# A spectral mixer and a Mish MLP on one core: early dense blocks on half chunks, loads reordered, planner given tile shapes and POOL durations

## The chip, the core and the metric

The kernel runs on one core of one Trainium2 chip. The metric is the time of one execution in microseconds as the device counts it, median over runs. The engines are PE (TensorE, matmuls; its weight loads are shown as PEld), DVE (VectorE), ACT (ScalarE), POOL (GpSimd) and SP (SyncE, which here only issues transfers). Transfers are issued from SP, ACT and POOL. PSUM, where PE writes, has eight banks of 512 float32 columns.

## The reference

Both branches read the same `x`, 2048 x 512 in bf16; a gate per row mixes them.

```python
x = A_x
g = _sigmoid((x * gate_w).sum(-1, keepdims=True))
a = _A_ref(x, A_w_r, A_w_i)     # irfft2(rfft2(x) * (w_r + 1j * w_i)), bf16
b = _B_ref(x, B_w1, B_b1, B_w2) # h = x @ w1 + b1 (512 -> 1792); act = h * tanh(softplus(h)); act @ w2
return g * a + (1 - g) * b
```

## The kernel before

**Tiling.** The 2048 rows are 16 tiles of 128 rows, in four chunks of four. `xo` holds the tiles as loaded, `xT` their transposes (made by PE against `ident`, L539, and copied out of PSUM by the tasks `evx`, L543). Everything stays in on-chip memory but two round trips of the spectral branch through DRAM (`scr1`, `scr2`).

**Dense branch.** For each chunk c and each of 14 blocks of 128 hidden units (ft), task `mm1_c_ft` is four matmuls of 512 columns (L861) into one PSUM bank, `mish` (L875, ACT) applies the activation out of that bank, and `mm2` (L892) multiplies by `w2`. The four blocks ft = 0 to 3 of chunk 0 ("early") are split in two tasks of two matmuls, `a` and `b`, by the halves of the contraction, because their `w1` comes in two pairs of loads (`ld_w1_a`, `ld_w1_b`). `DENSE` and `DENSE2` list the banks that mm1 and mm2 of a chunk may use.

**Spectral branch.** `t` (L561) forms sums and differences of `xT` into `Tb` (part of the buffer `Tg`) for a chunk; `a1` (L577) transforms along the row with the table `FDs` (load `ld_fd`); `eg`, `e1` (L584 to L595) combine into `Abuf`; `s1` (L608) is the first half of the transform down the columns, with 64-row tiles of PE and the tables `m1g1`; `e2` evicts to `Ybuf`, and `r1w` stores to `scr1`, one half issued from SP, the other from POOL. `r1r` (`Abuf<-scr`) reads back; `s2c`, `s2` (L704, L749: 64 rows by 32 columns), products with the spectral weights `WT` (`wm`, `wz`), `s2i` (L780: 32 by 64), stores and loads through `scr2`, then `s1i`, `a1i` (L809, L821) and the last sums. Small things on the side: `wcols` (POOL, L645) takes columns of `WT`, `rcw` (PE, L654), `weff` (DVE), `wab1` and `wab2` (POOL, L667 to L682) make a table from them; `gdot`, `gpow` (POOL, L631), `gcol`, `omg` make the gate.

**The order is made by a planner.** Every piece of work is a task with an engine, a duration, what it reads and writes, and a priority. `schedule()` walks through simulated time and picks among the ready tasks by priority plus a seeded noise (`SEED`, `MORE`). `LAND` gives times at which the first loads are taken to land. The result is one fixed order for each engine; each engine runs its order strictly in turn, and waits on semaphores where a task needs another engine's result. So a late input holds up everything that stands behind it on that engine. The planner's durations are assumptions: they set the order, not the time.

**The start.** The idle matmuls `warm` (L484) multiply constants while the first loads come in; nothing reads their result. The loads of tiles 0 to 3 are issued first, alternately from SP and ACT, then the first pair of `w1`, `b1`, `FD`, the second pair of `w1`, and the larger ones (tiles 4 and 5, tiles 6 and 7, `w1` blocks 4 to 7, ...).

Of the kernel before, what the change touches and what calls it, by code (L numbers as in the profile page):

```python
# [7 lines left out]
BF = mybir.dt.bfloat16  # L8
F32 = mybir.dt.float32
AF = mybir.ActivationFunctionType  # L10
ALU = mybir.AluOpType
# [105 lines left out]
class _Task:  # L117
    __slots__ = ("name", "eng", "dur", "fn", "deps", "lat", "sem", "semval", "idx", "sig",
                 "start", "done", "succ", "bl", "prio", "xfer", "opts", "isdma", "alloc", "frees", "lock", "nd")

    def __init__(self, name, eng, dur, fn, lat=0.0, prio=0.0):
# [20 lines left out]
        self.lock = False  # L142


SCH = dict(eps=0.03, sync=0.05)
# [3 lines left out]
class _Graph:  # L149
# [49 lines left out]
    def schedule(self):  # L199
# [26 lines left out]
        left = len(tasks)  # L226
        while left:
# [45 lines left out]
            ready.remove(t)  # L273
            t.start = est
# [48 lines left out]
S1N = 2  # L323
S1B = [(6, 7), (4, 5), (2, 3)]
A1B = (3, 4, 5, 6, 7)
SEED = 102926
NOISE = 0.02
MORE = (906649, 669565, 727213, 734900, 722035, 224221, 575189, 474236, 545212, 216745, 750436, 520841, 226433, 475143, 916690, 739973, 998134, 850898, 920291, 410068, 968422, 18581, 591859, 602267, 674493, 703441, 110116, 413622, 829488, 66903, 591144, 731731, 191705, 399980, 537679, 776088, 374283, 444805, 454649, 718084, 219781, 617544, 95571)
# [5 lines left out]
LAND = dict(ld_x0=2.9, ld_x1=3.1, ld_x2=3.7, ld_x3=4.0, ld_w1_a0=4.9, ld_w1_a1=5.0,  # L334
            ld_b1=6.6, ld_fd=5.6, ld_w1_b0=6.2, ld_w1_b1=6.2, ld_x4=9.0, ld_x6=9.0,
            ld_w1_4_0=10.0, ld_w1_4_1=10.6, ld_x8=12.1, ld_m10=13.1, ld_x12=14.4, ld_w1_8_0=15.3,
            ld_w1_8_1=16.0, ld_m11=17.3, ld_w1_12_0=17.7, ld_w1_12_1=18.1, ld_gw=18.5, ld_sm=19.0,
            ld_gd=19.3)
# [3 lines left out]
def _build(nc, A_x, A_w_r, A_w_i, B_x, B_w1, B_b1, B_w2, gate_w, out):  # L342
# [8 lines left out]
    with es:  # L351
# [128 lines left out]
        one_w, one_m = (nc.const_aps.tensor(1.0, (128, n), BF) for n in (128, 256))  # L480
        pw = _Ps([6])
        tw = []
        for i in range(NWARM):
            tw.append(pe(f"warm{i}", mm(256), lambda e: e.matmul(ps[:, pw.bank, 0:256], one_w, one_m, start=True, stop=True),  # L484
                         alloc=pw if i == 0 else None, frees=[pw], prio=0.0, deps=tw[-1:]))
# [46 lines left out]
        for t0, w in ((0, 1), (1, 1), (2, 1), (3, 1), (4, 2), (6, 2), (8, 2), (10, 2), (12, 2), (14, 2)):  # L532
            pt = _Ps(SPEC[::-1])
            def f_tr(e, t0=t0, w=w, pt=pt):
                ins = None
                for i in range(w):
# [8 lines left out]
                  reads=[("ptr", t0)], writes=[("xT", t0 + i) for i in range(w)], frees=[pt], engs=("dve",), prio=PR["tr"] + max(0, 4 - t0) * 0.2)  # L545
# [10 lines left out]
        for t in range(NT):  # L556
            if t % 4 == 0:
                G.cur_prio = PR["sp"] + 0.9
                h = t // 4
                cols = slice(512 * h, 512 * h + 512)  # L560
                for (nm, o, op) in (("s", 0, ALU.add), ("d", 2, ALU.subtract)):  # L561
                    tt(f"t{nm}{h}", lambda o=o, hb=h % 2: Tb[:, hb, o:o + 2, :], lambda cols=cols: xT[:, 0:2, cols],
                       lambda cols=cols: xT[:, 2:4, cols], op, 1024, rate=2.0,
                       reads=[("xT", 4 * h + i) for i in range(4)], writes=[("T", h % 2, nm)])
            if t % 2 == 0:
# [3 lines left out]
                for half in range(2):  # L569
# [11 lines left out]
                    pe(f"a1{half}_{t}", 4 * mm(128), f_a1, reads=[("T", hb, "s"), ("T", hb, "d"), "FD"], writes=[("pa", t, half)], alloc=pa,  # L581
# [14 lines left out]
            if t % 4 == 3:  # L596
                p1s = [_Ps(S1B) for _ in range(2)]
                for qd in range(0, 2, S1N):
# [13 lines left out]
                    s1_tasks.append(pe(f"s1_{tps[0]}", 4 * S1N * mm(256) + 0.22, f_s1, reads=[("In1" + x, tp) for tp in tps for x in "pmf"] + [("m1g1", t // 8)],  # L612
                                       writes=[("p1", tp) for tp in tps], alloc=p1s[qd:qd + S1N], prio=PR["sp"] + 0.4))
                for tp, p1 in zip((t - 3, t - 1), p1s):
# [3 lines left out]
                    for rho in range(2):  # L618
                        dma(f"r1w{tp}{'ab'[rho]}", scr1_w[rho][:, 2 * tp:2 * tp + 4, :], Y1[rho::2, 2 * tp:2 * tp + 4, :], reads=[("Y1", tp)],
                            writes=[("scr1", tp, rho)], nbytes=64 * 4 * 512, prio=PR["sp"] + 1.0, tail=0.7, bw=290e3, queue=("sp", "pool")[rho], issue=0.64)  # L620
# [10 lines left out]
        G.add("gpow", "pool", 0.3, lambda e: e.tensor_tensor(out=gcol[:, :], in0=omg[:, :], in1=gdot[:, :], op=ALU.pow),  # L631
# [32 lines left out]
        G.add("weff", "dve", 0.4, f_weff, reads=["pW"] + WALL, writes=["wq"], frees=[pW])  # L664
# [19 lines left out]
        G.add("wab2", "pool", 1.2, f_wab2, reads=["ch"], writes=["wab"], lock=True)  # L684
# [23 lines left out]
        pe("s2c", 0.6, f_s2c, reads=[("In2", r, u) for r in range(2) for u in range(8)] + ["sm"], writes=["pc"], alloc=pc)  # L708
# [29 lines left out]
        for v in range(4):  # L738
            u0, zb = 2 * v, v % 2
            q_of = {}  # L740
            for c in range(2):
# [11 lines left out]
                pe(f"s2_{v}{c}", mm(512) + 0.2, f_s2, reads=[("In2", r, u0 + i) for r in range(2) for i in range(2)] + ["sm"],  # L753
# [30 lines left out]
            t_s2i = pe(f"s2i_{v}", 2 * mm(512) + 0.25, f_s2i, reads=[("Z", zb, 2)] + [("Z", zb, r, c) for c in range(2) for r in range(2)] + ["sm"],  # L784
# [66 lines left out]
        for c in range(NCH):  # L851
            hb = c % 3
            G.cur_prio = PR["mm1"] - c
            for ft in range(NFT):
# [3 lines left out]
                def f_mm1(e, c=c, ft=ft, pd=pd, ds=range(4)):  # L858
                    ins = None
                    for i in ds:  # L860
                        ins = e.matmul(ps[:, pd.bank, :], w1_sb[:, i, 128 * ft:128 * (ft + 1)], xT[:, i, 512 * c:512 * c + 512],  # L861
                                       start=(i == 0), stop=(i == 3))
# [164 lines left out]
```

## Time and profile before

| what | us |
|---|---|
| median of 3 runs (131.64, 132.22, 132.03) | 132.03 |
| the profiled execution | 131.42 |
| its span, first to last instruction | 129.7 |
| PE busy in it | 126.3 |
| DVE, ACT, POOL busy | 87.8, 73.1, 63.8 |
| span of the last matmul's end to the span's end | 2.3 |

The granted TensorE clock is full in the mean over the span. The busy time of each engine by stretch of the span (PE, PEld, DVE, ACT, POOL; the counts in brackets are instructions; then the granted clock, the mean share in which the DMA engines were busy, and GB/s):

```profile
4.80:6.07 1.27, 1.05 (x12) 0.67 (x12) 1.23 (x5) 0.46 (x2) 0.00 (x0) 1.00 1.03 338
6.07:9.97 3.90, 3.88 (x30) 1.98 (x30) 1.59 (x4) 1.75 (x3) 0.00 (x0) 1.00 0.95 282
9.97:42.20 32.23, 32.23 (x266) 18.16 (x266) 29.11 (x59) 25.38 (x43) 10.74 (x21) 1.00 0.87 257
42.20:52.78 10.58, 10.54 (x50) 4.61 (x48) 4.57 (x14) 8.53 (x13) 7.67 (x12) 1.00 0.57 172
52.78:93.00 40.22, 40.22 (x307) 16.00 (x308) 23.56 (x22) 18.69 (x26) 21.76 (x25) 1.00 0.44 144
93.00:127.40 34.40, 34.40 (x269) 20.06 (x266) 26.98 (x56) 17.24 (x34) 22.43 (x30) 1.00 0.21 80
```

The first stretch is the end of the start-up, the second the first dense blocks, the third the rest of the forward spectral stage with dense work between, the fourth the round trip through `scr1`, the fifth the middle of the spectral branch, and the last the inverse transform with `mm2` between. A busy PE here counts pipelined matmuls that overlap, so the stretches are read by their lengths. DVE and ACT are busiest in the third.

### The profile page before, as it was taken

The numbers are of one execution on the slowest core, as the hardware profiler recorded it, in microseconds if no ns is written. First come the engines' busy times: TensorE is split into PE (matmuls) and PEld (weight loads), VectorE is DVE, ScalarE is ACT, GpSimd is POOL, SyncE is SP. The second block draws the span as 40 slices with busy tenths as digits, with TensorE's granted clock in tenths as the row PEclk, the third lists the DMA queues.
The fourth block names the chain that finished last, engine by engine and source line by source line (L and its number), as shares of the span: only waits on it lengthen the run. The fifth ranks groups of instructions, "written<-read, shape, count | busy, mean of one in ns | idle before, by whom it ended". The sixth has DMA issues, their size and how long they took to land.

```text
span 129.7 us, 2516 instructions
## 1 busy us (share of the span) xinstructions
PE 126.3 (97%) x948; PEld 64.3 (50%) x948; DVE 87.8 (68%) x157; ACT 73.1 (56%) x120; POOL 63.8 (49%) x97
## 2 busy tenths in 40 slices
PE   7999999999999999999999999999999999999992
PEld 5655756544455444344343333344556666555452
DVE  0638897988999921581698994600248987798672
ACT  0456567889887877604056857922245636743320
POOL 3000009800157994049579979200009887977820
PEclk9999999999999999999999999999999999999999
DMA  3999963999976645937014050465920030024213
GB/s 100 315 273 419 376 206 68 365 290 223 233 206 194 174 124 153 407 107 303 5 34 130 0 162 5 126 197 138 407 102 5 30 134 0 5 81 164 81 40 121
DMA packets 14584, 21.09 MB, mean 163 GB/s; under 512 B 1324, under 2 KB 10796, under 8 KB 14188
## 3 DMA queue, kind: packets, MB, share of 16 engines
q1 hardware_dynamic: 12288, 14.80, 34.3%
q0 software_dynamic: 1248, 4.99, 14.4%
q10 hardware_dynamic: 1036, 1.15, 2.8%
q8 instruction: 7, 0.11, 0.4%
q14 instruction: 5, 0.04, 0.1%
HBM read 14.64 MB, written 6.29 MB: 161 GB/s over the span
## 4 chain that ended last, share of the span: by engine, by line
PE 86%; DMA 5%; POOL 4%; DVE 1%; ACT 1%; issue 1%; SPq 0%
PE ps L892 37%; PE ps L861 29%; DMA Abuf<-scr 3%; PE ps L809 3%; PE ps L577 3%; PE ps L821 3%; PE ps L539 3%; PE ps L484 2%; POOL wab L674 2%; PE ps L608 2%; PE ps L749 2%; PE ps L780 2%; DMA scr<-Ybuf 2%; POOL scr L429 1%; DVE xT L459 1%; ACT Ybuf L460 1%
## 5 line engine op out<-in xcount | busy, mean ns | idle before, releaser
L861 PE MATMUL ps<-xT,w_sb 128*128 128x512 bf16 x224 | 52.8, 380 | 0.2 <-DVE xT L459 0.2
L892 PE MATMUL ps<-w_sb,act 128*128 128x512 bf16 (+2 forms) x238 | 51.6, 367 | 0.0
L875 ACT ACTIVATE act<-ps,b1f 128x512 bf16<-128x512 f32 x56 | 38.4, 687 | 15.0 <-PE ps L861 11.8
L892 PEld LDWEIGHTS ps<-w_sb,act 128*128 128x128 bf16 x238 | 21.9, 98 | 22.3 <-issue 0.6
L861 PEld LDWEIGHTS ps<-xT,w_sb 128*128 128x128 bf16 x224 | 19.9, 98 | 25.1 <-issue 2.6
L464 POOL TENSOR_TENSOR Tg<-Qb 128x256 bf16<-128x256 f32 x30 | 22.4, 773 | 19.9 <-DVE Qb L832 19.6
L464 POOL TENSOR_TENSOR Zb<-Qb 128x510 bf16<-128x510 f32 x16 | 19.8, 1267 | 8.3 <-DVE Qb L464 8.3
L464 DVE TENSOR_TENSOR Qb<-ps,WT 128x1024 f32<-128x1024 f32 x16 | 18.8, 1218 | 7.2 <-PE ps L749 4.1
L842 ACT ACTIVATE xo<-ps,omg 128x512 bf16<-128x512 f32 x14 | 9.6, 687 | 21.3 <-PE ps L892 20.5
L832 DVE SCALAR_TENSOR_TENSOR Qb<-ps,gcol,Qb 128x256 f32<-128x256 f32 x32 | 13.7, 475 | 3.0 <-PE ps L809 1.0
L464 DVE TENSOR_TENSOR Abuf<-ps,Tg 128x512 bf16<-128x512 f32 x16 | 10.3, 687 | 2.8 <-ACT Tg L584 2.2
L459 DVE CAST Ybuf<-ps 128x1024 bf16<-128x1024 f32 x8 | 9.8, 1222 | 3.3 <-PE ps L780 2.9
L459 DVE CAST Zb<-ps 128x512 bf16<-128x512 f32 x6 | 4.1, 688 | 11.5 <-PE ps L809 11.2
L826 ACT ACTIVATE Qb<-ps,gcol 128x256 f32<-128x256 f32 x16 | 7.3, 472 | 7.0 <-PE ps L821 7.0
L626 DVE SCALAR_TENSOR_TENSOR Tg<-xo,Tg 128x512 bf16<-128x512 bf16 x16 | 11.0, 686 | 0.4
L429 POOL DMA_DIRECT2D scr<-Ybuf x8 | 5.1, 645 | 12.0 <-ACT Ybuf L460 12.0
L429 POOL DMA_DIRECT2D w_sb<-in_B_w_dram x2 | 2.1, 1059 | 17.6 <-DMA sm<-c_sm 17.6
L460 ACT ACTIVATE Ybuf<-ps 128x1024 bf16<-128x1024 f32 x8 | 8.2, 1024 | 4.4 <-PE ps L780 3.3
L459 DVE COPY xT<-ps 128x1024 bf16<-128x1024 bf16 (+1 forms) x10 | 5.5, 582 | 5.3 <-PE ps L539 5.1
L464 DVE TENSOR_TENSOR xo<-xo,Tg 128x512 bf16<-128x512 bf16 x14 | 8.6, 644 | 0.6 <-POOL Tg L464 0.6
L821 PEld LDWEIGHTS ps<-GDs,Zb 128*128 128x128 bf16 x64 | 4.6, 98 | 2.6 <-DVE Qb L832 0.3
L821 PE MATMUL ps<-GDs,Zb 128*128 128x128 bf16 x64 | 5.9, 219 | 0.0
(68 smaller groups left out, 89.1 us busy)
## 6 DMA issues: line engine op xcount, KB each, us to landing
Abuf<-scr SPq DMA_DIRECT2D x8, 512.0 KB, 5.4
scr<-Ybuf SPq DMA_DIRECT2D x4, 512.0 KB, 3.2
w_sb<-in_B_w_dram POOLq DMA_DIRECT2D x2, 896.0 KB, 6.8
out_dram<-xo SPq DMA_DIRECT2D x6, 256.0 KB, 2.0
WT<-in_A_w_r_dram POOLq DMA_DIRECT2D x4, 257.0 KB, 9.0
WT<-in_A_w_i_dram POOLq DMA_DIRECT2D x4, 257.0 KB, 12.6
w_sb<-in_B_w_dram SPq DMA_DIRECT2D x4, 256.0 KB, 8.0
xo<-in_A_x_dram SPq DMA_DIRECT2D x2, 512.0 KB, 8.3
```

The costliest lines, as they stand in the source:

```text
L429: t = G.add(name, queue, issue, lambda e: e.dma_start(dst, src), reads=reads, writes=writes, lat=tail, deps=deps, prio=prio)
L459: fs = {"dve": ("dve", dve_dur(n, rate=rate), lambda e: e.tensor_copy(out=dst(), in_=src())), "act": ("act", act_dur(n), lambda e: e.activ ...
L460: "act": ("act", act_dur(n), lambda e: e.activation(dst(), src(), AF.Copy))}
L464: f = lambda e: e.tensor_tensor(out=o(), in0=i0(), in1=i1(), op=op)
L626: lambda e, t=t: e.scalar_tensor_tensor(out=junk, in0=xo[:, t, :], scalar=1.0, in1=gwb, op0=ALU.mult, op1=ALU.mult, accum_out=gdot[:, t:t ...
L821: ins = e.matmul(ps[:, p5.bank, 128 * i:128 * i + 128], TT[:, sl, 2 * par + ri, :], GDs[:, i, :], start=True, stop=True)
L826: lambda e, t=t, sl=sl, p5=p5: e.activation(gC[:, sl, :].rearrange("p (i n) -> p i n", i=2), ps[:, p5.bank, :].rearrange("p (i n) -> p i n ...
L832: lambda e, t=t, sl=sl, p5=p5, o=o, op=op: e.scalar_tensor_tensor(out=st1[:, sl, o::2, :], in0=ps[:, p5.bank, :].rearrange("p (i n) -> p i ...
L842: G.add_multi(f"bev_{t}", [("act", act_dur(512, True), lambda e: e.activation(xo[:, t, :], ps[:, pd.bank, :], AF.Copy, scale=omg[:, t:t + ...
L861: ins = e.matmul(ps[:, pd.bank, :], w1_sb[:, i, 128 * ft:128 * (ft + 1)], xT[:, i, 512 * c:512 * c + 512], start=(i == 0), stop=(i == 3))
L875: lambda e, ft=ft, pd=pd, hb=hb: e.activation(act[:, hb, ft, :].rearrange("p (t a b) -> p t a b", t=4, b=2), ps[:, pd.bank, :].rearrange(" ...
L892: ins = e.matmul(ps[:, pd.bank, cs_], act[:, hb, ft, 128 * tl:128 * (tl + 1)], w2_sb[:, ft, cs_], start=(ft == 0), stop=(ft == NFT - 1))
```

## The change

It has five parts.

1. **Early dense blocks by halves of the chunk.** Each of the four early blocks becomes four tasks of two matmuls with 256 columns: `a0`, `b0` (tiles 0 and 1) and `a1`, `b1` (tiles 2 and 3). They need only their two tiles. The sums and differences `t` of the first chunk are split in the same way, and `a1` waits for its half. Tiles 2 and 3 may be evicted by ACT too.
2. **Load order.** Tiles 0 and 1, the first pair of `w1`, tiles 2 and 3, the second pair of `w1`, then `b1` (ACT) and `FD` (SP). What follows is as before.
3. **Idle matmuls.** 36 of 128 columns, not 17 of 256.
4. **The planner.** It knows which tasks use other tile shapes of PE (`MODES`): it adds 0.095 us where the shape changes, prefers a task of the same shape that is nearly ready, and the allowances in the durations of `s1`, `s2`, `s2c`, `s2i` go. `gpow`, `wab2` and `weff` get 3.0, 3.1 and 0.9 us where they had 0.3, 1.2 and 0.4. `LAND`, the seeds and the assumed tail of the `r1w` stores are new.
5. **Banks.** mm1 of chunk 3 may use banks 0, 1 and 7, where it had 0 and 1; the first four transposes go through banks 4 to 7.

```diff
+MODES = {"s1": 1, "s2": 2, "s2c": 2, "s2i": 3}
+SWITCH = 0.095
...
+            stay = [c for c in cand if c[2][2] == "pe" and c[1].mode == mode and mode and c[0] <= free["pe"] + 0.15]
+            if stay:
+                cand = [c for c in cand if c[2][2] != "pe"] + stay
...
+            if t.eng == "pe" and t.mode != mode:
+                mode = t.mode
+                est += SWITCH
...
-DENSE = {0: (0, 1, 2), 1: (0, 1), 2: (0, 1, 7), 3: (0, 1)}
+DENSE = {0: (0, 1, 2), 1: (0, 1), 2: (0, 1, 7), 3: (0, 1, 7)}
...
-NWARM = 17
+NWARM = 36
...
-        one_w, one_m = (nc.const_aps.tensor(1.0, (128, n), BF) for n in (128, 256))
+        one_w, one_m = (nc.const_aps.tensor(1.0, (128, n), BF) for n in (128, 128))
...
-        for t in range(4):
+        for t in range(2):
             ld_x(t, t + 1, both[t % 2])
         ld_w1c(0)
+        for t in range(2, 4):
+            ld_x(t, t + 1, both[t % 2])
+        ld_w1c(1)
         dma("ld_b1", braw[:, :], B_b1.rearrange("(ft p) -> ft p", p=128), writes=["braw"], nbytes=3584, queue="act")
         dma("ld_fd", FDs[:].rearrange("p r k -> p (r k)"), d_FD[:], writes=["FD"], nbytes=131072)
-        ld_w1c(1)
...
-            pt = _Ps(SPEC[::-1])
+            pt = _Ps((7, 6, 5, 4) if t0 < 4 else SPEC[::-1])
...
-                  reads=[("ptr", t0)], writes=[("xT", t0 + i) for i in range(w)], frees=[pt], engs=("dve",), prio=PR["tr"] + max(0, 4 - t0) * 0.2)
+                  reads=[("ptr", t0)], writes=[("xT", t0 + i) for i in range(w)], frees=[pt], engs=("dve", "act") if t0 in (2, 3) else ("dve",), prio=PR["tr"] + max(0, 4 - t0) * 0.2)
...
+                for js in (((0,), (1,)) if h == 0 else ((0, 1),)):
+                    j0, nj = 256 * js[0], 256 * len(js)
+                    cols = slice(512 * h + j0, 512 * h + j0 + nj)
...
-        G.add("gpow", "pool", 0.3, lambda e: e.tensor_tensor(out=gcol[:, :], in0=omg[:, :], in1=gdot[:, :], op=ALU.pow),
+        G.add("gpow", "pool", 3.0, lambda e: e.tensor_tensor(out=gcol[:, :], in0=omg[:, :], in1=gdot[:, :], op=ALU.pow),
...
-        G.add("wab2", "pool", 1.2, f_wab2, reads=["ch"], writes=["wab"], lock=True)
+        G.add("wab2", "pool", 3.1, f_wab2, reads=["ch"], writes=["wab"], lock=True)
...
-                    t_a = pe(f"mm1_{c}_{ft}a", 2 * mm(512), lambda e, f=f_mm1: f(e, ds=(0, 1)), reads=xs + wr[0], alloc=pd, prio=PR["mm1"] - 0.06 * ft)
-                    pe(f"mm1_{c}_{ft}b", 2 * mm(512), lambda e, f=f_mm1: f(e, ds=(2, 3)), reads=xs + wr[1], writes=[("pm", c, ft)], deps=[t_a],
-                       prio=PR["mm1"] + 0.5 - 0.06 * ft)
+                    t_a = None
+                    for j in range(2):
+                        for h in range(2):
+                            tk = pe(f"mm1_{c}_{ft}{'ab'[h]}{j}", 2 * mm(256), lambda e, f=f_mm1, h=h, j=j: f(e, ds=(2 * h, 2 * h + 1), j0=256 * j, j1=256 * j + 256),
+                                    reads=xs[2 * j:2 * j + 2] + wr[h], writes=[("pm", c, ft, j)], alloc=None if t_a else pd, deps=[t_a] if t_a else (),
+                                    prio=PR["mm1"] + 0.8 * j + 0.3 * h - 0.06 * ft)
+                            t_a = t_a or tk
```

What the new plan makes of it, as the built programs have it (names of before in brackets where a line number would differ):

```
PE before: warm x14, transposes of tiles 0-3, warm x3, dense 512 x6, transpose of b1, dense x2, a1 x16, dense x4,
           transposes of tiles 6, 7 x8, dense x2, of tiles 4, 5 x8, dense x10, of tiles 8-11, ...
PE after:  warm x26, transposes of tiles 0, 1, warm x10, dense 256 x4, transposes of tiles 2, 3, dense 256 x6, a1 x8,
           transpose of b1, dense 256 x6, a1 x8, dense 256 x12, transposes of tiles 4-7, dense 256 x4, dense 512 x8,
           of tiles 8-11, dense x4, s1 x16 (L608), transposes of tiles 12-15, ...
s1 blocks: before, all four follow the transposes and the last a1; after, the first one as above, the others as before.
PE between the last s1 block and the first s2: before 48 dense matmuls; after rcw (L654) and 48 dense.
Dense (mm1) matmuls of 512 columns ahead of the first s2: before 164; after 156, two halves counted as one.
POOL before: w2 x2, WT x8, r1w x4, wcols, r1w x2, wab1, wab2, r1w x2, gpow, ...
POOL after:  r1w x2, w2 x2, WT x8, r1w x2, wcols, r1w x4, wab1, wab2, gpow, ...
```

More of the change, by code (lines that the diff above doesn't have):

```diff
@@ L782, in f_s2i @@
                 return ins
[L784 removed]
+            t_s2i = pe(f"s2i_{v}", 2 * mm(512) + 0.04, f_s2i, reads=[("Z", zb, 2)] + [("Z", zb, r, c) for c in range(2) for r in range(2)] + ["sm"],
                writes=[("p3", v)], alloc=p3)
@@ L877, in _build @@
                                                                           AF.Mish, bias=b1f[:, ft:ft + 1]),
-                      reads=[("pm", c, ft), "b1f"], writes=[("act", hb, ft)], frees=[pd], prio=PR["mish"])
+                      reads=([("pm", c, ft, j) for j in range(2)] if early else [("pm", c, ft)]) + ["b1f"], writes=[("act", hb, ft)], frees=[pd], prio=PR["mish"])
             G.cur_prio = PR["mm2"] - c
```

48 lines of the change are left out of this document (25 added, 23 removed).

## The prediction

> **What bounds the kernel now.** I read the page first: one engine is busy throughout.
>
> ```profile
> span 129.7 us, 2516 instructions
> PE 126.3 (97%) x948; PEld 64.3 (50%) x948; DVE 87.8 (68%) x157; ACT 73.1 (56%) x120; POOL 63.8 (49%) x97
> ```
>
> A busy PE need not be a PE at its rate, so next came the chain of waits in order of time (start, length, what).
>
> ```profile
> 0.83 3.15 PE ps L484 x14
> 3.98 0.44 PE ps L539 x4
> ...
> 4.87 1.16 DVE xT L459 x3
> 6.03 0.04 issue
> 6.07 1.47 PE ps L861 x6
> ...
> 9.97 0.62 PE ps L539 x8
> ...
> 27.37 3.45 PE ps L861 x16
> ...
> 42.66 3.06 POOL wab L674 x7
> 45.72 0.65 POOL scr L429
> 46.37 2.21 DMA scr<-Ybuf
> ...
> 48.66 4.08 DMA Abuf<-scr
> 52.74 0.04 issue
> 52.78 0.63 PE ps L749 x16
> ...
> 75.42 4.60 PE ps L861 x20
> ```
>
> Sixteen dense matmuls take 3.45 us, so 0.216 us each, and PE holds that rate nearly everywhere. What it loses lies in four places. (1) The start: nothing useful but sixteen transposes runs before 6.07, because the first dense block needs all four tiles evicted by DVE. (2) At 9.97, where transposes wait for a load. (3) At 52.78: the 48 dense matmuls in front began at 42.21, 48 x 0.216 = 10.37 gives 52.58, and the chain there runs through POOL and two transfers; of the 0.20 lost, 0.10 is the change of tile shape (below) and 0.10 the wait. (4) Small holds: twenty matmuls at 75.42 take 4.60, not 4.32. A block before a change of tile shape costs 0.10 more (eight take 1.83 at 33.76, in front of L608, and 1.73 at 17.81); the other 0.18 are two holds, and the timeline of the weight loads names the releaser, three times in this stretch.
>
> ```profile
> 70.33 0.55 PEld L861 LDWEIGHTS ps<-xT,w_sb 128*128 128x128 bf16 x4 [0.41 <-ACT act L875]
> ...
> 77.17 0.55 PEld L861 LDWEIGHTS ps<-xT,w_sb 128*128 128x128 bf16 x4 [0.41 <-ACT act L875]
> ...
> 78.98 0.55 PEld L861 LDWEIGHTS ps<-xT,w_sb 128*128 128x128 bf16 x4 [0.41 <-ACT act L875]
> ```
>
> So the kernel is a string of PE work from 6.07 to 127.4, and a change is worth what it takes off the front or out of the string. The list of loads gives the arrival times.
>
> ```profile
> FDs<-c_fd SPq DMA_DIRECT2D x1, 128.0 KB, 3.9
> xo<-in_A_x_dram ACTq DMA_DIRECT2D x1, 256.0 KB, 6.6
> ```
>
> FD is issued at 2.17 and lands at 6.11; tiles 6 and 7 are issued at 3.29 and land at 9.92. The landing events give the rest: tiles 0 and 1 at 3.59 and 3.79, 2 and 3 at 4.78 and 5.08, the first w1 pair at 5.53 and 5.74, the second at 6.45 and 6.77, w1 blocks 4 to 7 at 11.28.
>
> **The change, part by part.** *Idle matmuls.* Fourteen of 256 columns last from 0.83 to 3.77, 0.210 each; 26 of 128 columns take 26 x 0.105 = 2.73 and end at 3.56. Tile 0 lands at 3.59, so its transposes start near 3.60, 0.17 earlier. Evictions follow as before: the second ended at 4.87 + 0.42 = 5.29, now 5.12, and PE starts 0.06 later (as 6.01 to 6.07): first dense matmul at 5.18. The first w1 pair must be there: it takes the queue places of tiles 2 and 3, 5.08. The ten idle matmuls in between (three slow, seven at 0.056, from 4.46) end at 5.17 and cost nothing. So dense work starts 0.89 earlier, but eight transposes (tiles 2, 3) now stand behind it: 8 x 0.056 = 0.45. Lead 0.44.
>
> *Halved early matmuls.* 16 more matmuls and weight loads. Four 128-column ones take 0.22 against 0.216 for one of 512, under 0.003 for each extra start: 0.04 in all. The extra weight loads (0.098 each) hide under matmuls of 0.109; where that cover is thinner, in the 0.056 transposes, they hide too.
>
> *Load order.* The second w1 pair is now seventh and eighth of the 128 KB loads, FD ninth. The eighth landed at 6.45, the tenth at 6.77. PE wants w1 at 5.18 + 0.44 + 0.45 + 0.44 = 6.51 and FD at 6.73. Bounds 0 to 0.26 of waiting; I take 0.05, since the places say 6.45 and between 6.45 and 6.77. DVE's four half-size sums (0.35 each, from 5.12) end at 6.5 and are covered too; one eviction moves to ACT, idle then.
>
> *The next loads cap the lead.* Up to tiles 6 and 7 PE has 14 half pairs x 0.219, 8 + 16 transposes and line transforms x 0.056 and 0.21 for the small transpose = 4.63; 5.18 + 4.63 + 0.05 = 9.86. Tiles 6 and 7 land at 9.92, so these transposes start at 9.97 again. Before, PE had done 12 full dense matmuls by then and waited 0.18; now 14. Lead 2 x 0.216 = 0.43, less 0.01 for the halves left: 0.42. Then w1 blocks 4 to 7 are needed at 11.30 and land at 11.28. Both loads stand where they stood, with the same bytes ahead. Bounds 0.34 (PE 0.26 late) to 0.47.
>
> *The order behind.* The built program has the same groups of each tile shape (four of L608, nine of the others), so the knowledge of shapes saves no change of 0.10: nothing. The first L608 block moves up to before the last transposes; DVE must have made its input by 14.9. From 4.3 it has about 9.0 us to do (its operations at 0.61, the half-size ones at 0.35), end 13.3; if not, PE waits in order and everything behind it. POOL's wab now stands behind the stores: 3.06 off a chain that had missed by 0.10; the loads land some 3 us early. Gain 0.10. The last dense chunk gets a third bank: the three holds go, 0.26 (bounds 0 to 0.26). Chunk 1 keeps two banks, and ACT has an extra eviction (1.02) and copies before it: I allow two holds of 0.09, 0.17 (bounds 0 to 0.26). Behind 127.41 nothing changes.
>
> Sum: -0.42 - 0.10 - 0.26 + 0.17 = -0.61 (the cost of the halves is in the 0.219). The profiled execution took 131.42, its span 129.7 and 1.7 around it, and the median of the runs is 0.61 above that. So 131.42 - 0.61 = 130.81 for an execution like the profiled one, and on the median 132.03 - 0.61 = **131.4**.
>
> **Rivals.** *B, the good ends.* Start 0.47, wait 0.10, holds 0.26 and none new: -0.83, 131.2. For it: ACT runs its evictions 0.59 apart back to back (7.96, 8.55), so it need not be late. Against: two loads must land sooner than they did.
>
> *C, PE still slow when dense work begins.* The transposes of tile 1 ran 0.107 apart, those of tile 2, at 4.82, 0.056: the clock rose at 4.81, and dense now starts only 0.37 later. Had it risen later, the old kernel would hardly mind before 6.07; the new one loses half of each us from 5.18 on, at most 0.45. Then 0.61 - 0.45 = 0.16 is left: 131.9. The Trainium skill ("TensorE: Matmul & The Clock Gate", Part 1) states that the window is free-running and the rise comes around 4 us into matmul activity, give or take 0.5 us from run to run. By that rule the rise would be at 4.3 to 5.3 and cost at most 0.06; the trace's 3.98 us after the first matmul agrees.
>
> *D, slower: the spectral weights come late.* The first L608 block's four stores (0.52 MB) now run at 17 to 20, ahead of w2 and the WT tables, on POOL's queue too. WT's last piece landed at 38.05, wcols takes 0.75 on POOL, and its matmuls (rcw) stand in PE's order right behind the last L608 block. Eight dense matmuls fewer precede that, so PE is there at about 42.1 - 1.73 - 0.42 = 40.0. From WT at 39.2 on PE stands, one us for each. Price: nothing, if the stores fill the slack in which DMA is 30% to 60% busy (slices at 16 to 22 us); all 0.52 MB at WT's own 2.06 MB in 16.5 us would be 4.2 late, a stall of 3.0. In the middle 1.5, net 1.5 - 0.61 = +0.9: 132.9. It is slower than before once WT is 0.6 later than 39.2. Against: w2 waits for sm at 19.16 anyway. The Trainium skill ("DMA: Bandwidth & Descriptors", section "Issuing engines are not separate DMA queues") says that all issuing engines share the same 16 DMA engines. By that rule moved stores would push the loads; no row prices this pair.
>
> *That it does not do what it says* holds for the shapes alone; by the built order the dense blocks do start on tiles 0 and 1.
>
> **How the numbers follow.** The sum 0.55, its own range 131.2 (holds all gone) to 131.8 (start 0.34, two more holds); as 0.61 is just short of 0.66, a good third of it, 0.20, lies beyond. B 0.18, C 0.12, D 0.15. A measurement of this kernel tells 0.5%, 0.66 us, from no change. Faster by more: 0.20 + 0.18 = 0.38; within: 0.35 + 0.12 = 0.47; slower: 0.15. The range takes in B with the scatter of the runs (0.4 below the median), C, and D's smaller prices: 130.8 to 132.5.
>
> **What would show it.** First dense matmul at 5.2 with w1 landed at 5.1; transposes of tiles 6 and 7 still released by their load near 9.95; the first dense matmul of block 4 at 11.3, not 11.74; no DMA in front of L749's counterpart; no weight load of the last chunk held by ACT; last matmul at 126.8. It is wrong if PE stands in front of rcw or the first L608 block, or if dense matmuls run 0.21 apart at 256 columns after 5.2.

## The result and the profile after

The changed kernel takes 132.44 us (median of 22 runs, 131.75 to 133.83), the kernel before 131.80 in as many runs on the same chip (131.16 to 132.84). The ratio is 1.0056, with an interval of 1.0035 to 1.0077: slower by 0.6%, where 0.5% faster had been forecast. All ratios here leave out runs more than 1.5% above the fastest of the same kernel, and they are not quotients of the medians. The profiled execution took 132.13, 0.71 more than that of before, so the two profiles show a difference of the size of that of the medians, 0.64. Both lie below the medians of their kernels, by 0.31 and by 0.38.

The head of the page of the changed kernel: the span and the engines' busy time.

```profile
span 130.4 us, 2586 instructions
PE 126.5 (97%) x983; PEld 67.4 (52%) x983; DVE 89.6 (69%) x165; ACT 72.5 (56%) x116; POOL 62.8 (48%) x95
```

PE is as busy as before and the span is 0.7 longer: the string of PE work begins later, or has a hole. The chain of waits in order of time (start, length, what) shows where; L877, L593, L552, L624 and L765 are what L861, L577, L539, L608 and L749 were.

```profile
2.65 5.11 DMA FDs<-c_fd
7.76 0.14 issue
7.90 0.61 PE ps L593 x8
...
11.14 0.89 PE ps L552 x16
...
41.19 0.20 PE ps L670
...
41.41 10.47 PE ps L877 x48
51.87 0.56 PE ps L765 x16
...
75.21 5.29 PE ps L877 x24
...
104.91 0.40 PE ps L837 x4
```

The chain now starts with a load: FD, issued at 2.65, lands at 7.76. The transposes of tiles 4 to 7 start near 11.0, where the forecast had those of tiles 6 and 7 at 9.97. The middle is as forecast: nothing stands between the 48 dense matmuls and L765 (before, the chain ran through POOL operations and two transfers there), and 24 dense matmuls of the last chunk at 75.21 take 5.29, where 24 x 0.216 and 0.10 for the change of shape make 5.28; before, twenty had taken 4.60. The matmuls of the start, from the timeline of PE (start, length to the modelled end, line and count; in brackets the idle time before, with its releaser):

```profile
3.93 1.03 PE L552 MATMUL ps<-ident,xo 128*128 128x128 bf16 x8 [0.17 <-DMA xo<-in_A_x_dram]
4.76 1.11 PE L495 MATMUL ps<-const-bfloat16-1.0 128*128 128x128 bf16 x10
5.71 0.60 PE L877 MATMUL ps<-xT,w_sb 128*128 128x256 bf16 x4
6.14 0.61 PE L552 MATMUL ps<-ident,xo 128*128 128x128 bf16 x8
6.59 0.82 PE L877 MATMUL ps<-xT,w_sb 128*128 128x256 bf16 x6
7.90 0.61 PE L593 MATMUL ps<-FDs,Tg 128*128 128x128 bf16 x8 [0.49 <-DMA FDs<-c_fd]
```

Ten idle matmuls from 4.76 on keep PE until 5.71: 0.95, most of them at half clock (0.107 each), though the second eviction was done at 5.42. After six half-size matmuls from 6.59 (6 x 0.109 gives 7.24) PE stands 0.66 for FD. It then does not see tiles 4 to 7 late at all (the last of them landed at 10.08).

Put in one row, how far PE's work stands behind the profiled execution of before, at the same task: 0.58 after the first dense blocks, 0.75 in front of the last chunk of mm1, 0.47 behind it, 0.71 at the end. The steps between are the two new holds in chunk 1 (0.06 and 0.08), a wait in front of `rcw` (0.09: L670 starts 1.08 after the s1 block's first matmul, where 0.99 is what it takes), the wait gone at L765 (0.10 gained), the holds gone in chunk 3 (0.28 gained), and one wait in front of L837 (0.23 lost). In sum 0.58 + 0.14 + 0.09 - 0.10 - 0.28 + 0.23 = 0.66; 0.05 is spread in smaller pieces. The last of these waits, in the timeline of the weight loads:

```profile
104.91 0.23 PEld L837 LDWEIGHTS ps<-GDs,Zb 128*128 128x128 bf16 x4 [0.24 <-DVE Qb L848]
```

So four fifths of the difference between these two executions arise in the first 8 us, and there the forecast rested on landing times and on a clock that one profile had shown once.

### The profile page after: what moved, and what is told of

It is laid out like the page before. It is cut to its first block, busy times and chain, and to the rows that moved or that the text cites. A ratio compares the mean times of both kernels' runs of the same rounds, so it can differ in the third digit from the quotient of the medians.

```text
span 130.4 us, 2586 instructions
## 1 busy us (share of the span) xinstructions
PE 126.5 (97%) x983; PEld 67.4 (52%) x983; DVE 89.6 (69%) x165; ACT 72.5 (56%) x116; POOL 62.8 (48%) x95
## 4 chain that ended last, share of the span: by engine, by line
PE 91%; DMA 4%; SPq 1%; DVE 1%; issue 1%; ACT 0%; DVEq 0%
PE ps L877 37%; PE ps L914 36%; DMA FDs<-c_fd 4%; PE ps L624 3%; PE ps L837 3%; PE ps L593 3%; PE ps L825 2%; PE ps L552 2%; PE ps L765 2%; PE ps L796 2%; SPq L440 1%; DVE Qb L848 1%; ACT Qb L842 0%; DVE xo L926 0%; PE ps L670 0%
## 5 line engine op out<-in xcount | busy, mean ns | idle before, releaser
L877 PE MATMUL ps<-xT,w_sb 128*128 128x512 bf16 (+1 forms) x240 | 52.4, 365 | 0.0
L877 PEld LDWEIGHTS ps<-xT,w_sb 128*128 128x128 bf16 x240 | 21.8, 98 | 23.6 <-issue 1.9
L475 POOL TENSOR_TENSOR Tg<-Qb 128x256 bf16<-128x256 f32 x28 | 20.9, 774 | 19.7 <-DVE Qb L848 19.5
L470 DVE CAST Zb<-ps 128x512 bf16<-128x512 f32 x8 | 5.5, 685 | 11.5 <-PE ps L825 11.2
L475 DVE TENSOR_TENSOR Abuf<-ps,Tg 128x512 bf16<-128x512 f32 x16 | 10.4, 685 | 1.3 <-ACT Tg L600 0.9
L475 DVE TENSOR_TENSOR xo<-xo,Tg 128x512 bf16<-128x512 bf16 x14 | 8.1, 615 | 0.8 <-ACT xo L858 0.8
L837 PEld LDWEIGHTS ps<-GDs,Zb 128*128 128x128 bf16 x64 | 4.7, 98 | 3.1 <-DVE Qb L848 0.2
L837 PE MATMUL ps<-GDs,Zb 128*128 128x128 bf16 x64 | 6.0, 219 | 0.1
L471 ACT ACTIVATE Zb<-ps 128x512 bf16<-128x512 f32 x8 | 4.7, 595 | 2.6 <-PE ps L825 2.6
```

Of the source, the lines that this page charges most:

```text
L470: fs = {"dve": ("dve", dve_dur(n, rate=rate), lambda e: e.tensor_copy(out=dst(), in_=src())), "act": ("act", act_dur(n), lambda e: e.activ ...
L471: "act": ("act", act_dur(n), lambda e: e.activation(dst(), src(), AF.Copy))}
L475: f = lambda e: e.tensor_tensor(out=o(), in0=i0(), in1=i1(), op=op)
L837: ins = e.matmul(ps[:, p5.bank, 128 * i:128 * i + 128], TT[:, sl, 2 * par + ri, :], GDs[:, i, :], start=True, stop=True)
L877: ins = e.matmul(ps[:, pd.bank, j0:j1], w1_sb[:, i, 128 * ft:128 * (ft + 1)], xT[:, i, 512 * c + j0:512 * c + j1], start=(cnt[0] == 0), st ...
```

## The experiments

All of them keep the order of the changed kernel (or of the kernel before) on every engine, as its planner made it, and edit that order. `first(eng, names)` puts the named loads at the head of an engine's order, `line(names)` puts the named tasks of PE in this order into the places that they hold, and `later(names, ahead_of)` moves tasks of PE to just ahead of another. The code is cut to the lines that make the change. The kernel before was run beside each batch on the same chip, and ratios are to it; the unchanged new kernel (c2) ran beside the second batch alone, so the other variants are compared with it across chips. Two theories were open at first. A: the load order itself costs, since FD became the last of the early loads. B: PE is slow at the start, and where it idles there its clock comes later. After the first batch came C: the last of the first ten loads lands at 6.7 to 8.6, whichever it is, and the changed PE order asks for FD and the second w1 pair too early. (The ten are nine of 128 KB and the small b1, whose landing the profiles do not record in full; the times are those of the nine.) Rival D of the prediction, WT late, was taken up later, when its wait turned up in profiles.

**1. The load order.** e3 gives the kernel before the new order of loads; e2 gives the changed kernel the old one; e1 moves FD alone, ahead of the second w1 load on SP. c1 is the kernel before once more, for a second profile.

```diff
 # e3 (kernel before): the changed load order
+first("sp", "ld_x0 ld_w1_a0 ld_x2 ld_w1_b0 ld_fd".split())
+first("act", "ld_x1 ld_w1_a1 ld_x3 ld_w1_b1 ld_b1".split())
 # e2 (changed kernel): the old load order
+first("sp", "ld_x0 ld_x2 ld_w1_a0 ld_fd ld_w1_b0".split())
+first("act", "ld_x1 ld_x3 ld_w1_a1 ld_b1 ld_w1_b1".split())
 # e1 (changed kernel): FD earlier
+first("sp", "ld_x0 ld_w1_a0 ld_x2 ld_fd ld_w1_b0".split())
+first("act", "ld_x1 ld_w1_a1 ld_x3 ld_w1_b1 ld_b1".split())
```

Expected of e1: 

> The changed kernel with every engine's order kept; only the line-transform table FD goes ahead of the second w1 load on SP's queue. Theory A (load order: FD came last, landed at 7.76 and PE stood 0.66 us in front of the first line transform): FD lands at 6.2 to 6.6, no PE wait over 0.1 there, 0.5 to 0.65 us faster than the changed kernel, so 131.8 to 131.95, ratio to before 1.000 to 1.002. Theory B (PE clock: the clock rises late, 5.56 instead of 4.81, behind the shorter idle matmuls, and dense work and idle matmuls run at half rate): time as the changed kernel, 132.4, ratio 1.005.

Expected of e2: 

> The changed kernel with every engine's order kept, but the first ten loads in the order of before (tiles 0 to 3, first w1 pair, FD and b1, second w1 pair). Theory A: first dense matmul waits for w1 until 5.6 to 5.9, about as late as it started at 5.71, FD at 6.1 to 6.4, no wait of 0.66: 131.8 to 132.0, ratio 1.000 to 1.002. Theory B: 132.4, ratio 1.005.

Expected of e3: 

> The kernel before with every engine's order kept, but its first ten loads in the changed order. Theory A: tiles 2 and 3 land at 5.3 to 5.5 instead of 4.8 to 5.1, first dense matmul at 6.4 to 6.5 instead of 6.07, FD (7.8) just in time for the line transforms at 8.4: 0.35 to 0.4 us slower than before, ratio 1.003. Theory B: idle matmuls are as before, so the clock is, and the time stays within 0.1 us: ratio 1.000.

Expected of c1: 

> The kernel before, unchanged, for a second profile. If the first load's landing (3.59 before, 3.88 after) and the rise of the clock (4.81 before, 5.56 after) scatter from run to run, they differ here by some 0.2 to 0.7 us from the first profile; if the change made them, they stand within 0.1 us of it.

Measured: e3 1.0007 (0.9992 to 1.0022), e2 1.0044 (1.0017 to 1.0071), e1 1.0072 (1.0041 to 1.0103). A falls three times: the new load order costs the old kernel nothing, the old one does not save the changed kernel, and FD ahead of the second w1 load only made that load the last (7.65 in e1's profile, FD at 6.66). All three ratios are what B had forecast, and two profiles show B's side. In e1's, PE waited only 0.1 for `w1` and not for FD, but tile 0 landed at 4.21 and the matmuls ran at half rate until 6.4; PE ended 0.66 behind the first profile of before all the same. In e2's, an execution of 133.89, the granted clock rose only at 9.95. c1's profile (132.32, 0.90 more than the first one of the same kernel) shows that the times which the prediction had taken were not the kernel's, but one execution's. Its PE timeline:

```profile
6.30 1.02 PE L861 MATMUL ps<-xT,w_sb 128*128 128x512 bf16 x4 [0.63 <-DMA w_sb<-in_B_w_dram]
8.13 0.59 PE L861 MATMUL ps<-xT,w_sb 128*128 128x512 bf16 x2 [0.80 <-DMA w_sb<-in_B_w_dram]
```

The first w1 pair landed at 6.16 and the second at 7.99; in the profile that the prediction was read from they landed at 5.74 and 6.77, and neither was waited for.

**2. What competes with the early loads.** The last of the early loads is under way together with the load of tiles 6 and 7 (256 KB, issued from ACT at 3.29 before). e4 issues that one from SP, behind tiles 4 and 5; e5 does the same in the kernel before; e6 is e4 without the ten idle matmuls behind the transposes of tile 1. c2 is the changed kernel again.

```diff
 # e4, e5, e6: tiles 6 and 7 from SP, behind tiles 4 and 5
+x6 = next(t for t in order["act"] if t.name == "ld_x6")
+order["act"].remove(x6)
+x6.eng = "sp"
+order["sp"].insert(6, x6)
 # e6 and e9: without the idle matmuls behind the transposes of tile 1
+order["pe"][:] = [t for t in order["pe"]
+                  if not (t.name.startswith("warm") and int(t.name[4:]) >= 26)]
```

Expected of e4: 

> The changed kernel with every engine's order kept; only the load of tiles 6 and 7 (256 KB) is issued from SP behind that of tiles 4 and 5, not from ACT, so that FD shares the transfer engines with no large load. Theory C: FD lands at 6.8 to 7.1, the wait in front of the first line transform is under 0.2, tiles 6 and 7 land up to 0.4 later (10.0 to 10.3): 0.3 to 0.5 us faster than the changed kernel, ratio 1.000 to 1.003. Theory B (late clock alone): ratio 1.004 to 1.007 as without it.

Expected of e5: 

> The kernel before with the same move of the load of tiles 6 and 7. Theory C: its last load (second w1 pair, 6.77 in one profile and 7.99 in the other) lands at 6.5 to 7.0 in every run, so runs with a wait of 1.2 us there go: median 0.1 to 0.3 us lower, ratio 0.998 to 0.999, less scatter. Theory B: ratio 1.000.

Expected of e6: 

> As the run with tiles 6 and 7 on SP, and without the ten idle matmuls behind the transposes of tile 1 (26 are left). Theory C with the idle matmuls on PE's path (first dense matmul could start at 5.48 but stood behind them until 5.71, and until 6.15 instead of 5.8 in the run with FD early): 0.1 to 0.3 us faster than that run, ratio 0.998 to 1.002. Theory B (the clock rises only behind a stretch in which PE was busy throughout): PE idles for 0.6 to 0.8 us before the first dense matmul, the rise comes up to 3.4 us later in a part of the runs, as in the run with the old load order (9.95): ratio 1.006 or more, wide scatter.

Expected of c2: 

> The changed kernel, unchanged, for a second profile and its time on this chip. Theory C (whichever of the first ten loads is last lands at 6.7 to 8.6, and the changed order of PE needs both the second w1 pair and FD by 6.7, where the order before needed FD only after 8): FD lands after 7 again and PE stands in front of the first line transform, or the clock is late; ratio 1.004 to 1.007. If FD lands before 6.8 and the clock rises before 5 and the run is still 0.5 us slower, C is wrong.

Measured: c2 1.0054 (1.0028 to 1.0081), e4 1.0019 (0.9993 to 1.0044), e5 0.9997 (0.9974 to 1.0019), e6 1.0008 (0.9977 to 1.0038). By the middle values e4 recovers two thirds of the loss, as C had it, though the intervals still overlap; e5 changes nothing, which is B's number and not C's. e4's one profile does not show what the move was made for: FD landed at 7.63, not at 6.8 to 7.1, and PE stood 0.67 for it, as long as in the changed kernel. (The timeline names a DVE operation there, but PE starts 0.14 behind FD's landing in this profile as in the first after, c2, e6, e9 and e11.) c2's profile has FD at 7.89 and a wait of 0.55 for it, as C had it. In e6's profiled execution (131.25) FD, the second w1 pair and the clock (4.12) came as early as the prediction had counted on, though tile 0 (4.04) did not. Its PE timeline:

```profile
5.33 0.61 PE L877 MATMUL ps<-xT,w_sb 128*128 128x256 bf16 x4 [0.63 <-DVE xT L470]
5.78 0.61 PE L552 MATMUL ps<-ident,xo 128*128 128x128 bf16 x8
6.23 0.82 PE L877 MATMUL ps<-xT,w_sb 128*128 128x256 bf16 x6
6.89 0.61 PE L593 MATMUL ps<-FDs,Tg 128*128 128x128 bf16 x8
```

FD landed at 6.75, PE came to it at 6.89, and dense work was 0.44 ahead of the first profile of before: a lead of the size that the prediction worked out exists, when the loads come. But the twelve runs of e6 reach from 131.25 to 134.68, those of e4 from 131.33 to 132.78. Such a spread is what B had expected of a PE that idles; the ratio, 1.0008, is what C had expected. And e6 lost 0.22 of its lead again in front of `rcw`.

**3. Asking later, or idling less.** e7 moves the first two a1 tasks and the small transposes to later in PE's order; e8 also puts all first-half matmuls in front, takes e4's loads and leaves five of the ten idle matmuls; e9 is the changed kernel without the ten.

```diff
 # e7
+later(("a10_0", "a11_0", "tr_small"), ahead_of="a10_2")
 # e8: e4's loads, warm31 and above left out, and PE's order behind the transposes of tiles 2, 3:
+line("mm1_0_1a0 mm1_0_3a0 mm1_0_0a1 mm1_0_1a1 mm1_0_2a1 mm1_0_3a1 mm1_0_0b0 mm1_0_0b1 a10_0 a11_0 tr_small "
+     "mm1_0_1b0 mm1_0_1b1 a10_2 a11_2 mm1_0_2b0 mm1_0_2b1 mm1_0_3b0 mm1_0_3b1".split())
```

Expected of e7: 

> The changed kernel; PE does the first two a1 tasks (L577) and the small transposes just ahead of the third a1 task, some 0.9 us of dense matmuls later; nothing else moves. Theory C (the last of the first ten loads lands at 6.7 to 8.6, and the changed PE order asks for FD at 6.7 to 7): the wait of 0.66 in front of the first a1 shrinks below 0.1 wherever FD lands by 8, the transposes of tiles 6 and 7 start about 0.5 earlier, at 10.4 to 10.6, ratio to before 1.000 to 1.003. Theory B (PE slow at the start, the loads hide behind it): the wait goes, but only in runs whose clock is up by 5.6; ratio 1.004 to 1.006, as the changed kernel.

Expected of e8: 

> The changed kernel; all first-half-contraction matmuls (a0, a1) of the early blocks ahead of the b ones, a1 of L577 behind those of the first block, tiles 6 and 7 loaded from SP behind tiles 4 and 5, five of the ten idle matmuls behind the transposes of tile 1 left out. Nothing then needs the second w1 pair before about 7.4 or FD before about 7.9. Theory C: no wait for these loads, transposes of tiles 6 and 7 at 9.9 to 10.2, ratio 0.995 to 0.999, a version ahead of both kernels. Theory B: the runs spread by when the clock rises, median 0.999 to 1.002. If the loss lay behind the start (the new stall of 0.23 in front of L837 and others), 1.002 to 1.005 whatever the start does.

Expected of e9: 

> The changed kernel without the ten idle matmuls behind the transposes of tile 1. They ran at half clock, 0.107 each, and held the first dense matmul back by 0.2 to 0.4. Theory C: FD is waited for in any case, so dense work starts 0.2 earlier and waits 0.2 longer; ratio 1.004 to 1.006. If these idle matmuls are the loss: 1.001 to 1.004. Theory B, a PE that idles gets its clock later: 1.005 to 1.008, with some runs over 133.

Measured: e7 1.0025 (1.0000 to 1.0051), e8 1.0009 (0.9984 to 1.0033), e9 1.0018 (0.9984 to 1.0052; the median of all its twelve runs is 132.48 against 131.74). e7's ratio is C's, but its medians, 132.31 against 131.74, are as far apart as B had it, and its profile is not what C expected: the second w1 pair landed at 7.57 in that execution and was waited for (0.40 in brackets; PE stood 0.57, until 7.70), and the transposes started at 11.2, not at 10.4 to 10.6. e8 waited for no load, and stood 0.50 for its own order instead, all a1 halves wanting tiles 2 and 3, whose eviction on ACT ended late; it did not get ahead of both kernels as C had it, and 1.0009 is B's number. e9 is between the expectations, and its runs spread from 131.24 to 133.50. In e9's profile, too, PE stood 0.68 for FD.

e7 and e9 showed something else. The chain of waits of e9, in order of time, leads through WT:

```profile
26.43 13.42 DMA WT<-in_A_w_i_dram
...
40.01 0.71 POOL wrv L661
...
41.00 0.26 POOL wrv L662
41.26 0.05 issue
41.31 0.20 PE ps L670
```

PE had ended the s1 block at 40.83 and stood 0.48 for `rcw`, whose columns POOL could take from WT only once that had landed (39.85). In the nine profiles of the changed kernel and its variants up to e9 this wait was 0.48 (e9), 0.22 (c2, e6, e7), 0.09 (the first), and none in e1, e2, e4 and e8. It stands where rival D had it, at prices from 0 to 0.5, not 3.0, but the late WT is only half of it. The other half is how long POOL takes for the four copies of `wcols`: 0.72 in all four profiles of the order of before, and 0.72 to 1.71 here. In e6, WT had landed at 38.40; the copies and two DVE operations that ran beside them (start, length):

```profile
38.56 0.69 POOL L661 COPY wrv<-WT 128x2 bf16<-128x2 bf16 x1 [1.36 <-DMA WT<-in_A_w_i_dram]
39.19 0.32 POOL L662 COPY wrv<-WT 128x30 bf16<-128x30 bf16 x1
39.35 0.66 POOL L661 COPY wrv<-WT 128x2 bf16<-128x2 bf16 x1
39.95 0.31 POOL L662 COPY wrv<-WT 128x30 bf16<-128x30 bf16 x1
...
38.52 0.68 DVE L642 SCALAR_TENSOR_TENSOR Tg<-xo,Tg 128x512 bf16<-128x512 bf16 x1
39.24 0.71 DVE L642 SCALAR_TENSOR_TENSOR Tg<-xo,Tg 128x512 bf16<-128x512 bf16 x1
```

In e8 the two copies of L661 take 0.19 and 0.18; the long ones here end 0.05 behind the DVE operation that was under way when they began (spans on POOL are rough). In the sixteen profiles thirteen of these copies are long (over 0.35), and each began under such a DVE operation (`Tg<-xo,Tg`) and ended 0.05 or 0.18 behind it. Had the copies taken 0.72, they would have ended before the s1 block did in all five profiles with a wait, in e6 0.81 before. No run moves these DVE operations, so this stands on the traces alone. The loads of WT in the list of transfers, before (first fence) and after (KB each, median us from issue to landing):

```profile
WT<-in_A_w_r_dram POOLq DMA_DIRECT2D x4, 257.0 KB, 9.0
WT<-in_A_w_i_dram POOLq DMA_DIRECT2D x4, 257.0 KB, 12.6
```

```profile
WT<-in_A_w_r_dram POOLq DMA_DIRECT2D x4, 257.0 KB, 12.1
WT<-in_A_w_i_dram POOLq DMA_DIRECT2D x4, 257.0 KB, 13.9
```

With the first s1 block's stores ahead, the first half takes 3.1 more and the second 1.3 more; the last piece landed at 39.27 where it had landed at 38.05. Over all profiles the difference is less clear: 38.05 to 39.62 with the order of before, 38.40 to 40.49 with the changed one.

**4. The parts apart, and together.** e11 is the changed kernel with `rcw` alone moved, behind four more dense matmuls. e10 has that and three more: tiles 6 and 7 from SP, five idle matmuls fewer, and an order of the early blocks by what they need. e12 is e10 with one DVE operation moved, the suspect of the 0.23 in front of L837.

```diff
 # e10, e11, e12
+pe_ = order["pe"]
+rcw = next(t for t in pe_ if t.name == "rcw")
+pe_.remove(rcw)
+pe_.insert(1 + next(i for i, t in enumerate(pe_) if t.name == "mm1_1_12"), rcw)
 # e10, e12: e4's loads, warm31 and above left out, and
+line("mm1_0_0a0 tr2 tr3 mm1_0_2a0 mm1_0_1a0 mm1_0_3a0 mm1_0_0b0 mm1_0_1b0 mm1_0_0a1 mm1_0_1a1 mm1_0_2a1 mm1_0_3a1 "
+     "mm1_0_0b1 a10_0 a11_0 tr_small mm1_0_1b1 a10_2 a11_2 mm1_0_2b0 mm1_0_2b1 mm1_0_3b0 mm1_0_3b1".split())
 # e12
+dv = order["dve"]
+sm0 = next(t for t in dv if t.name == "sum_0")
+dv.remove(sm0)
+dv.insert(1 + next(i for i, t in enumerate(dv) if t.name == "sap_5"), sm0)
```

Expected of e10: 

> The changed kernel with four moves: tiles 6 and 7 from SP behind tiles 4 and 5; five of the ten idle matmuls behind the transposes of tile 1 left out; the early blocks ordered by what they need (one block's a0, the transposes of tiles 2 and 3, the other a0, two b0, all a1, and only then FD's a1 of L577), so that the second w1 pair is needed at about 6.8 and FD at about 8.4; rcw behind four more dense matmuls, so that a WT up to 0.8 later holds nothing. If late loads and the wait for WT are the loss: transposes of tiles 6 and 7 at 9.9 to 10.3, no wait in front of rcw, ratio 0.994 to 0.998. If the scatter of PE's clock is the loss: median ratio 0.998 to 1.001, runs from 131.2 to 132.8. If the loss lies behind 45 us: 1.001 to 1.004.

Expected of e11: 

> The changed kernel with rcw (L670, L671) behind four more dense matmuls; nothing else moves. If rival D (WT late, PE standing in front of rcw) is part of the loss: the waits of 0.09 to 0.48 there are gone, ratio 1.002 to 1.004. If the loss is the start alone: what is waited for at rcw is 0.1 in the middle, ratio 1.004 to 1.006, as the changed kernel.

Expected of e12: 

> e10 with one DVE operation later: the sum of tile 0 (sum_0, 0.95) behind sap_5 instead of ahead of sam_4, so that the inputs of the seventh a1i task (L837) come some 0.9 earlier. If the 0.23 that PE stands there in every changed kernel is a loss of its own: it is gone, lead at the end 0.2 larger than e10's for the same start, ratio 0.995 to 0.998. If PE's time there is given back a few tasks on (another wait on DVE, whose work is as much as before): 0.997 to 0.999, as e10.

Measured: e11 1.0020 (0.9999 to 1.0041), 132.19 against 131.94; e10 0.9980 (0.9961 to 0.9999), 131.69 against 131.94; e12 0.9981 (0.9954 to 1.0008), 131.41 against 131.66.

e11 lies where a share of the wait at `rcw` in the loss puts it, though its interval overlaps that of the changed kernel, so the share is not measured to better than a few tenths of a us. Its profiled execution isolates the other part: the clock rose at 4.22, dense work began at 5.27, near the forecast of 5.18, and still it stood 0.38 behind the first profile of before when the early blocks were done, for FD. Its PE timeline:

```profile
4.48 0.75 PE L495 MATMUL ps<-const-bfloat16-1.0 128*128 128x128 bf16 x10
5.27 0.61 PE L877 MATMUL ps<-xT,w_sb 128*128 128x256 bf16 x4
5.72 0.61 PE L552 MATMUL ps<-ident,xo 128*128 128x128 bf16 x8
6.17 0.89 PE L877 MATMUL ps<-xT,w_sb 128*128 128x256 bf16 x6
7.70 0.61 PE L593 MATMUL ps<-FDs,Tg 128*128 128x128 bf16 x8 [0.65 <-DMA FDs<-c_fd]
```

So a PE at full clock does not help by itself: it comes to FD at 6.89 and stands 0.81, until 7.70. In e10 and e12 twenty dense matmuls stand between the transposes of tiles 2, 3 and the first use of FD. The timeline of e12's PE, of its start and around the place in question:

```profile
6.39 2.35 PE L877 MATMUL ps<-xT,w_sb 128*128 128x256 bf16 x20
8.57 0.61 PE L593 MATMUL ps<-FDs,Tg 128*128 128x128 bf16 x8
...
104.01 0.39 PE L825 MATMUL ps<-m1g,Abuf 128*128 128x128 bf16 x4
104.24 0.39 PE L837 MATMUL ps<-GDs,Zb 128*128 128x128 bf16 x4
```

Neither has a wait in brackets: FD and the second w1 pair (6.48) were there, and L837 follows L825 at 0.23, where in the first profile after it stood 0.45 behind. That removes the stall: e12's PE is 0.03 behind the first profile of before in front of this place and 0.03 behind at the end, while e10's goes from 0.13 ahead to 0.10 behind. It is not given back later. The ratios of e10 and e12 do not differ, though, so in the medians this 0.23 is not shown: e12's number is the one expected if that time were given back. e10's 0.998 lies on the border of two expectations, late loads and the scatter of the clock, and does not choose between them. WT landed at 39.58 in e12 and PE did not wait. The runs of both are the tightest of all variants of the changed kernel (131.20 to 132.03, 131.12 to 132.24). e10 is ahead of both kernels, by 0.2%, only just clear of the noise; e12's interval takes in no change. Part of the gain is still lost: in both profiles PE stands 0.27 in the middle of the transposes of tiles 4 to 7, until DVE has done with a PSUM bank of the late a1 tasks.

What the runs settle, then: e10 with its four moves takes the loss away (0.9961 to 0.9999, against 1.0028 to 1.0081 for c2), so it lies at the start and at `rcw`, where these moves are. How the loss of the medians divides between late loads (C), the late clock (B) and `rcw` is not shown: no ratio of a single move stands clear of the changed kernel's, and the profiles show each of the three.

## Why the prediction was wrong

**The step that failed** is in "Load order": PE wants the second w1 pair at 6.51 and FD at 6.73, the loads land at 6.45 to 6.77, "Bounds 0 to 0.26 of waiting; I take 0.05". The wait measured 0.66. PE's need was about right (7.24, and 6.71 once the later start is taken off), the landing was not: FD came at 7.76, 1.0 behind the latest time that the bounds allowed. In sixteen profiles of kernels that differ little at the start, the last of the first ten loads lands at 6.75 to 8.59, and the profile used had the second lowest value, 6.77; it was a lucky draw, at 131.42 against the kernel's median of 131.80. The bounds came from two landing events of one execution and were taken as the kernel's. PE stood 0.55 to 0.81 for FD in five profiles with the changed order (the first after, c2, e4, e9, e11). The kernel before needs FD only behind eight full dense matmuls, at 8.0 or later, and so had room for it: in e3 FD landed at 8.59, and PE came to it at 8.80 without a wait. The change used that room up. For the w1 pairs the kernel before has no such room: c1 waited for both, and ended 0.88 behind.

**A term left at nothing.** The ten idle matmuls "end at 5.17 and cost nothing" rested on a clock that rises at 4.8 and on tile 0 at 3.59. In the profile after, tile 0 landed at 3.88, the granted clock rose at 5.56, and seven of the ten ran 0.107 apart: dense work began at 5.71, 0.53 later than forecast; 0.29 of this is the load, 0.23 the idle matmuls, that stood until 5.71 when the evictions would have let PE go at 5.48. Together with the wait for FD (0.61 more than the 0.05 taken) that is 1.14, less 0.11 for the wait on tiles 6 and 7 that was then gone, 1.03; measured, the transposes came 1.01 later than forecast, at 10.98 and not at 9.97. This is most of the miss of the profiled execution, 0.71 + 0.61 = 1.32. The rest is the 0.23 in front of L837 and the 0.09 at `rcw`.

**Rival C** (clock late: 131.9) was of the right kind, but capped at 0.45 and thought of alone. Where FD is late anyway an early clock does not help (e11); and the cap was too low: in e2's profile the granted clock rose 3.5 behind the first dense matmul, and half of each us of that is 1.75. **Rival D** (WT late: 132.9) had the right place and half of the cause, and a middle price of 1.5 where 0 to 0.48 was measured. Its condition, WT later than 39.2, rested on 0.75 for `wcols`; e6 stood there with WT at 38.40, because the copies took 1.69. It is also a cap that the prediction had not seen: had the start come as forecast, PE would have been at `rcw` near 40.1, and e6, which was, stood 0.22 there.

**What held.** Start, when the loads come: lead 0.42 forecast, 0.44 in e6 (which has other edits too). Wait in front of L749 gone: 0.10, 0.10. Holds of the last chunk: 0.26, 0.28. Two new holds in chunk 1: 0.17, 0.14. No gain from the shapes, no wait in front of the first s1 block: both so. The 0.23 in front of L837 was not in the sum, which has no term for the inverse transform at all. In both kernels DVE does three sums of outputs there (2.15 and 2.20 in all) ahead of the operation that this a1i task needs, but before, 14 matmuls of `mm2` stood between this task and the a1i task ahead of it, and in the new order seven. The half-size idle matmuls and the planner's knowledge of shapes were not tried alone.

**The clock.** The first matmul starts at 0.83, and the spacing of matmuls goes from 0.107 to 0.056 (128 columns), with the granted clock, at 4.1 to 6.8 in the profiles, once at 9.95. The Trainium skill ("TensorE: Matmul & The Clock Gate", Part 1) has a free-running window of about 3.4 us, and so a rise that scatters by half a us from run to run. The scatter agrees, its width does not: 3.3 to 6.0 us after the first matmul, and 9.1 in the one at 9.95 (e2, where PE waited 0.61 for w1 in front of 6.45). The measurement decides, and the term for the clock should have had at least the bounds 4.1 to 6.8.

## What to carry to other kernels

A landing time from one profile is one draw: before work is moved towards a load, profile the same kernel twice or more, and ask how late the latest was, not whether this one was in time. Order work by when its inputs can be late: in e10 and e12 work that needs only what is there by 6.5 stands in front of the first use of FD, and neither profile has a wait for a load there; with three moves more, e10 turns a loss of 0.6% into a gain of 0.2%. And a lead won early is cashed only up to the next thing that comes at its own time (in e6 the columns of WT, ready at 40.26), so the waits behind have to be looked at with the lead subtracted.

## What was not expected of the hardware

The last of the nine early loads of 128 KB, all issued between 0.8 and 2.9, lands at 6.75 to 8.59. Where the next, larger load (256 KB) is issued from ACT right behind them, it lands at 6.77 to 8.59, with 7.8 in the middle (ten profiles); where that load goes to SP behind another, at 6.75 to 7.63, with 7.0 in the middle (six). So the load issued later seems to take from the earlier ones, though single profiles of the two groups overlap (6.77 and 7.63). The Trainium skill ("DMA: Bandwidth & Descriptors", section "Issuing engines are not separate DMA queues") says that transfers of all issuing engines interleave on the same 16 DMA engines; this agrees. The first load, issued at 0.80 in every profile, lands at 3.56 to 4.21.

Idle matmuls are not free: at half clock they stand in PE's order like any other (0.23 of the start here). Left out altogether they go with long runs (e6 and e9: five of 24 runs above 133.4 us). None of the 36 runs of e8, e10 and e12, which keep five of the ten, is above 133; but these differ in other ways too, and of the 87 runs of the kernels that keep all ten five are above 133.4 as well. That it is the clock in these long runs is not shown: the profiles of e6 and e9 have the rise at 4.12 and 5.31, and the only profile that fell on a long run is e2's.

Thirteen POOL copies of `wcols` that began while DVE did `Tg<-xo,Tg` took 0.37 to 0.84 in place of 0.18 to 0.32, and ended just behind that operation. Two others that began under one took 0.18 and 0.19.
